# Windowed attention and a gated MLP on one core: four one-bank accumulators, more idle products and another order of the pieces at the start

## The chip, the core and the metric

The kernel runs on one core of a Trainium2 chip. The metric is device time in microseconds (us) from one execution; the profile is of one further execution and has its own time. Engines: TensorE (PE; PEld is its weight load), VectorE (DVE), ScalarE (ACT), GpSimd (POOL) and SyncE (SP), which issues nearly all DMAs.

## The reference

Attention over 8 entries (B), 8 heads, 576 positions and 64 columns a head. Heads 0 to 3 see a plain window of 32 positions back; heads 4 to 7 see 32 positions back at a distance of 4 (dilated). The result is the input of an MLP with a sigmoid gate.

```python
scores = scale * np.matmul(q, k.transpose(0, 1, 3, 2))
mask_plain = (rel >= 0) & (rel < window)
mask_dil = (rel >= 0) & (rel < window * dilation) & (rel % dilation == 0)
scores = np.where(masks[None, :, :, :], scores, -1000000000.0)
...
attn = np.exp(scores)
attn = attn / (np.sum(attn, axis=-1, keepdims=True) + 1e-09)
return np.matmul(attn, v).astype(np.float32)
...
x = np.ascontiguousarray(attn_out.transpose(0, 2, 1, 3)).reshape(B * S, H * D)
h = x @ w_in
g = h * (1.0 / (1.0 + np.exp(-1.702 * h)))
return (g @ w_out).astype(np.float32)
```

x is 4608 x 512, w_in 512 x 2048, w_out 2048 x 512. The weights come as 64-bit floats.

## The kernel before

**Pieces and their order.** The body of the kernel adds pieces of work to a plan (`Plan.add`, L49): each has a cost on every engine that could do it, an urgency, the keys that it reads and writes, and at times a slack. `Plan.ordered` (L69) then writes out the order by hand: it keeps a clock for each engine and for the DMA bus, takes the engine that can start first, and on it the piece of the lowest urgency among those that can start. Pieces whose urgency is below 4 (the first entry's) may be preferred though they start later by `AHEAD` times the cost (L104 to 110). The engines then run their queues in this order, each strictly in order. The costs, urgencies, slacks, `AHEAD` and `WARM` are the planner's numbers, not measurements, and act on the order alone. What an instruction waits for is worked out apart from the plan, from the tiles that it reads and writes.

**Attention.** A pair of heads is one unit, 32 pairs in all, 4 to each entry. Pair k loads q and k (`load_qk`, L308) and v (`load_v`, L322), multiplies scores in small 32-row blocks (`scores`, L354: masks at L361, products at L375) into the tile sp, takes a softmax over a window of 64 (`exponentials` and `softmax`, L378 to 423: L394 maximum, L398 exponential, L412 sum, L421 or L425 transposes; GpSimd or VectorE divide), and multiplies by v. The first entry (pairs 0 to 3) has a way of its own: `first_attention` (L529) with `first_product` (L446, L462), which writes x into the accumulators' tile, as it is not yet in use; `drain_x` (L478) takes x out, a rounded high part xh by ScalarE and the rest xl by VectorE. Later pairs go by `attention` (L538) and `product` (L467, L476) through the tile av.

**MLP.** Tokens go in nine groups: 512 of each entry, and the rest of all entries in one. Every float32 factor is split in a high and a low part, and three products stand for one. A group has 16 steps f: `up` (L586) multiplies 12 times (L597: 4 blocks c of x, 3 products) into the bank hp; ScalarE's tanh (L605), VectorE's gate (L608), a rounding (L226) and a subtraction (L233) make gh and gl; `down` (L627) adds 12 products (L633, L634 for gh, L637 for gl) to four accumulators j of 128 x 512, one PSUM bank each. TensorE's order is up(f+1), then down(f). In the last step, each accumulator is drained (L645; L226 by ScalarE, tile ost) and stored when its three products are through. The next group's first `down` begins them anew, after its `up(1)`. All four accumulators are one tile:

```python
accs = bank([P, NC, GT], "acc", "acc")
```

**Weights.** `decode` (L241) turns one 128 x 512 block of 64-bit weights into a high and a low float32 part: one DMA (L271), ScalarE copies (L281, L282, at times L275), VectorE integer work (L277, L285, L287), a rounding (L226 or L228) and a subtraction (L233, VectorE or GpSimd). 32 blocks (n even: w_in, n odd: w_out) are decoded during the first entry and the first group.

**Idle products.** Before a piece on TensorE that the plan expects later than TensorE is free, up to its time `WARM`, the plan puts products of the identity with itself (L719), of which nothing is read, as many as fit by a formula (L116). They are written into the bank hp, and only until the first group's first `up` has used it.

**DMA.** All loads stand in SP's queue in the plan's order. At the start these are qk of pairs 0 to 3, the first blocks of weights and v of pairs 0 to 3.

Of the kernel before, what the change touches and what calls it, by code (L numbers as in the profile page):

```python
# [22 lines left out]
AHEAD = 0.6  # L23
WARM = 30.0
# [10 lines left out]
LATER = {PE: 0.0, ACT: 0.0, DVE: 0.4, POOL: 0.0, DMA: 0.0}  # L35
# [3 lines left out]
class Plan:  # L39
# [29 lines left out]
    def ordered(self, warm, warm_until, soon):  # L69
# [24 lines left out]
        while any(open_):  # L94
# [19 lines left out]
            if e == PE and when < warm_until:  # L114

                idle = max(0, int((when - max(free[e], 1.2) - 1.5) / (0.28 if when > 5.0 else 0.44)))  # L116
                order.extend([(None, e)] * idle)
# [20 lines left out]
def tile_windowed_attention_then_gated_mlp(  # L138
# [49 lines left out]
    accs = bank([P, NC, GT], "acc", "acc")  # L188
# [52 lines left out]
    def decode(n, urgency):  # L241
# [38 lines left out]
        add({DMA: 524}, {0: -7.0, 1: -5.0, 2: -3.5, 3: -2.5}.get(n, urgency), fetch, (), (R, R + "l", *taken))  # L280
# [41 lines left out]
    def load_v(k):  # L322
        u, place = pairs[k], lots(k)[1]

        def work(e):
            if k < NC:
                n = (QT if dilated(k) else QT + 1) * 2 * D
                flat = (None, late, main_x, left_x)[k][:, 2 * S:2 * S + n] if k else temp([P, n], F32, "v", f"v_{k}")
                u["v"] = flat.rearrange("p (s a d) -> p s a d", a=2, d=D)

                load(flat, first_v[k][:, 2 * D * (QT + 1) - n:])
                return
            flat = late_v if place == "v1" else temp([P, 2 * nv], F32, "v", f"v_{k}")
            u["v"] = [flat[:, nv * a:nv * a + nv].rearrange("p (m d) -> p m d", m=NW) for a in range(2)]
            for a in range(2):
                load(u["v"][a][0:KW], vp[k - NC, :, a])

        add({DMA: 390 if k < NC else 442}, (-5.5, -3.0, -2.0, -1.0)[k] if k < NC else 1.6 * k - 0.3, work, waits(k),
            (place, place + "l"), (0.0, 6.0, 8.0, 10.0)[k] if k < NC else 0.0)
# [66 lines left out]
    def softmax(k, urgency):  # L406
# [7 lines left out]
        for a in range(2):  # L414
            add({POOL: 0.73, DVE: -0.48}, urgency, lambda e, a=a: pair(
                e, pr[:, a], pr[:, a], sm[:, a, :, None].broadcast_to([P, QT, W]), ALU.mult), (SM,), (f"{PR}.{a}",))
# [29 lines left out]
    def first_product(k):  # L446
# [6 lines left out]
        u["x"] = accs[:, :, ROW * (k % 2):ROW * (k % 2) + ROW]  # L453
# [24 lines left out]
    def drain_x(k, urgency):  # L478
# [19 lines left out]
        if b == 0:  # L498
# [8 lines left out]
            for n, (size, part, src) in enumerate(mains):  # L507
                add({ACT: 0.12 + size * 0.00094}, urgency, lambda e, part=part, src=src: copy(
                    e, part(xh[:, c]), src()), FOUR, (f"xh{c}.{n}",))
                add({DVE: 0.08 + size / 640}, urgency, lambda e, part=part, src=src: pair(  # L510
                    e, part(xl[:, c]), src(), part(f32(xh[:, c])), ALU.subtract), (*FOUR, f"xh{c}.{n}"), (f"xl{c}.{n}",))
# [17 lines left out]
    def first_attention(k, urgency):  # L529
# [3 lines left out]
        add({PE: 1.7}, urgency - 1.0e5, lambda e: scores(k), (lots(k)[0],), ("sp",))  # L533
        softmax(k, urgency)
        add({PE: 1.1}, urgency - 1.0e5, lambda e: first_product(k), (lots(k)[1], f"ct{k % 2}.0", f"ct{k % 2}.1"), FOUR)
# [29 lines left out]
    class Group:  # L565
# [20 lines left out]
        def up(self, f):  # L586
# [12 lines left out]
            for c in range(NC):  # L599
                split = [f"x{k}{c}.{n}" for k in "hl" for n in range(1)] if self is main[0] else []  # L600
# [26 lines left out]
        def down(self, f):  # L627

            def hi(j):
                if f == 0:  # L630
                    self.acc[j] = accs[:, j]
# [53 lines left out]
    for c in range(NC):  # L685
        first_attention(c, c)
        if c in (1, 2):
            decode(c - 1, c + 2.5)
    last, nxt = None, 1
    for g in groups:  # L690
        g.split_x()
        if nxt == 1:
            for n in range(2, 2 * NF - 8):
                decode(n, 25.0 + 2.3 * n)
# [6 lines left out]
        for f in range(NF):  # L701
            g.up(f)
            if nxt == 1 and f == 1:
                for c in range(NC):
                    attention(NC + c, 50.0 + 10.0 * c)
                for n in range(2 * NF - 8, 2 * NF):
                    decode(n, 25.0 + 2.3 * n)
# [7 lines left out]
    def warm(e):  # L715
        if 0 not in main[0].hps:
            if "idle" not in misc:
                misc["idle"] = bank([P, GT], "hp", "idle")
# [49 lines left out]
```

## Time and profile before

| what | value |
|---|---|
| median of 3 runs | 924.18 us (923.68 to 924.65) |
| the profiled execution's own time | 923.53 us |
| its span, first to last instruction | 921.8 us |
| mean granted TensorE clock | 0.990 |
| DMA | 61.32 MB, mean 67 GB/s |

Three stages can be told apart in the windows view by busy time: up to 40 us, the first entry's attention and the first decodes, with VectorE at 27.75 us and ScalarE at 25.89; from there to about 130 us, the first group beside the remaining decodes and the second entry's attention, with DVE and ACT nearly full; then the other eight groups, with TensorE full and DVE and ACT less than half used. Times in the views count from the span's start. A row of the timeline is: start, length, engine, line, operation, output and inputs, count, and in brackets the idle time of the engine before it and what ended it. Matmuls are pipelined: the start of the next, not the length of a row, tells the rate. In a row of waits stand the total, the number and the longest.

### The profile page before, as it was taken

The numbers are of one execution on the slowest core, as the hardware profiler recorded it, in microseconds if no ns is written. First come the engines' busy times: TensorE is split into PE (matmuls) and PEld (weight loads), VectorE is DVE, ScalarE is ACT, GpSimd is POOL, SyncE is SP. The second block draws the span as 40 slices with busy tenths as digits, with TensorE's granted clock in tenths as the row PEclk, the third lists the DMA queues.
The fourth block names the chain that finished last, engine by engine and source line by source line (L and its number), as shares of the span: only waits on it lengthen the run. The fifth ranks groups of instructions, "written<-read, shape, count | busy, mean of one in ns | idle before, by whom it ended". The sixth has DMA issues, their size and how long they took to land.

```text
span 921.8 us, 17123 instructions
## 1 busy us (share of the span) xinstructions
PE 888.0 (96%) x7313; PEld 714.7 (78%) x7313; DVE 450.3 (49%) x844; ACT 386.0 (42%) x669; POOL 71.7 (8%) x86
## 2 busy tenths in 40 slices
PE   6899999999999999999999999999999999999997
PEld 4577777888788878888788878887888778878885
DVE  6799985564556254634564255525422412232221
ACT  5889874343543244323443244424422322232222
POOL 3312220010001000000010000100000000000000
PEclk9799999999999999999999999999999999999999
DMA  9366742211221012300311023101000010001001
GB/s 347 126 223 179 246 134 91 92 46 46 91 92 46 1 64 73 92 0 16 122 46 47 1 91 91 46 1 44 24 1 1 2 44 1 1 14 32 1 1 46
DMA packets 35803, 61.32 MB, mean 67 GB/s; under 512 B 17424, under 2 KB 17680, under 8 KB 35728
## 3 DMA queue, kind: packets, MB, share of 16 engines
q1 hardware_dynamic: 35584, 60.11, 20.3%
q8 instruction: 57, 0.93, 0.4%
q14 instruction: 18, 0.15, 0.1%
q10 hardware_dynamic: 144, 0.13, 0.0%
HBM read 49.48 MB, written 9.44 MB: 64 GB/s over the span
## 4 chain that ended last, share of the span: by engine, by line
PE 90%; ACT 5%; DMA 2%; DVE 1%; issue 1%; SPq 0%; ACTq 0%
PE hp_m L597 37%; PE acc L637 14%; PE acc L633 14%; PE acc L634 13%; PE hp_r L597 5%; PE av L476 3%; PE sp L375 3%; ACT ost_m L226 2%; DMA cell<-wo_dram 1%; PE acc L462 1%; DMA cell<-wi_dram 1%; DMA second<-wo_dram 1%; ACT words L281 1%; ACT second L275 1%; ACT gh L226 0%
## 5 line engine op out<-in xcount | busy, mean ns | idle before, releaser
L633 PE MATMUL acc<-gh,woh 128*128 128x512 f32 x576 | 226.9, 394 | 4.9 <-ACT ost_m L226 4.1
L634 PE MATMUL acc<-gh,wol 128*128 128x512 f32 x576 | 224.4, 390 | 0.0
L597 PE MATMUL hp_m<-xh,wih 128*128 128x512 f32 x512 | 203.8, 398 | 2.8 <-ACT xh L226 1.9
L597 PE MATMUL hp_m<-xl,wih 128*128 128x512 f32 x512 | 201.4, 393 | 0.3 <-DVE xl L233 0.2
L597 PE MATMUL hp_m<-xh,wil 128*128 128x512 f32 x512 | 201.3, 393 | 0.0
L608 DVE SCALAR_TENSOR_TENSOR g_m<-g_m,hp_m 128x512 f32<-128x512 f32 x128 | 87.8, 686 | 230.3 <-ACT g_m L605 229.9
L637 PE MATMUL acc<-gl,woh 128*128 128x512 f32 x576 | 162.3, 394 | 13.7 <-ACT ost_m L226 11.7
L605 ACT ACTIVATE g_m<-hp_m 128x512 f32<-128x512 f32 x128 | 76.6, 599 | 234.4 <-PE hp_m L597 233.9
L637 PEld LDWEIGHTS acc<-gl,woh 128*128 128x128 f32 x576 | 107.6, 188 | 44.3 <-ACT ost_m L226 19.0
L633 PEld LDWEIGHTS acc<-gh,woh 128*128 128x128 f32 x576 | 108.1, 188 | 31.1 <-ACT ost_m L226 6.1
L634 PEld LDWEIGHTS acc<-gh,wol 128*128 128x128 f32 x576 | 108.2, 188 | 21.9
L233 DVE TENSOR_TENSOR gl<-g_m,gh 128x512 fp32r<-128x512 f32 x126 | 89.1, 707 | 58.1 <-ACT gh L226 52.9
L597 PEld LDWEIGHTS hp_m<-xh,wih 128*128 128x128 f32 x512 | 97.0, 190 | 25.5 <-DVE g_m L608 3.1
L597 PEld LDWEIGHTS hp_m<-xl,wih 128*128 128x128 f32 x512 | 97.2, 190 | 22.1 <-DVE xl L233 1.4
L597 PEld LDWEIGHTS hp_m<-xh,wil 128*128 128x128 f32 x512 | 97.1, 190 | 20.1 <-POOL wil L233 0.6
L226 ACT ACTIVATE gh<-g_m 128x512 fp32r<-128x512 f32 x117 | 73.9, 632 | 68.8 <-DVE g_m L608 68.6
L233 POOL TENSOR_TENSOR pr<-pr,sm 128x320 f32<-128x320 f32 x64 | 52.4, 840 | 520.8 <-DVE sm L404 516.6
L226 ACT ACTIVATE bt<-ct 32x320 f32<-32x320 f32 x101 | 47.5, 470 | 14.3 <-DVE ct L425 12.4
L226 ACT ACTIVATE xm<-av 128x512 f32<-128x512 f32 (+2 forms) x42 | 24.5, 594 | 44.8 <-PE av L476 31.5
L608 DVE SCALAR_TENSOR_TENSOR g_r<-g_r,hp_r 128x512 f32<-128x512 f32 x16 | 11.0, 688 | 53.6 <-ACT g_r L605 53.6
L398 ACT ACTIVATE pr<-pr 128x640 f32<-128x640 f32 x32 | 23.7, 740 | 30.9 <-DVE pr L233 30.8
L412 DVE TENSOR_REDUCE sm<-pr 128x10 f32<-128x640 f32 x32 | 26.2, 817 | 13.3 <-ACT pr L398 13.3
(114 smaller groups left out, 717.6 us busy)
## 6 DMA issues: line engine op xcount, KB each, us to landing
qk<-qk_dram SPq DMA_DIRECT2D x17, 576.0 KB, 4.8
out_dram<-ost_m SPq DMA_DIRECT2D x31, 256.0 KB, 2.0
second<-qk_dram SPq DMA_DIRECT2D x13, 576.0 KB, 4.3
v<-vp_dram SPq DMA_DIRECT2D x32, 216.0 KB, 4.3
words<-vp_dram SPq DMA_DIRECT2D x24, 216.0 KB, 4.4
cell<-wi_dram SPq DMA_DIRECT2D x10, 512.0 KB, 5.6
cell<-wo_dram SPq DMA_DIRECT2D x9, 512.0 KB, 4.4
second<-wo_dram SPq DMA_DIRECT2D x6, 512.0 KB, 5.2
```

The source lines that it names most:

```text
L226: A.activation(dst, src, AF.Copy, scale=scale)
L233: (V if e == DVE else G).tensor_tensor(out=dst, in0=a, in1=b, op=op)
L375: T.matmul(dst[:, w:w + n], u["qk"][rows, at:at + 32], u["qk"][rows, S + first:S + first + n], start=not masked(k), stop=True, tile_positi ...
L398: add({ACT: 0.75}, urgency, lambda e: A.activation(prs[y], prs[y], AF.Exp, scale=0.125), (), (PR,))
L412: add({DVE: 0.80}, urgency, lambda e: V.tensor_reduce(out=sm, in_=pr, axis=AX.X, op=ALU.add), (PR,), (SM,))
L476: T.matmul(dst, u["v"][a][0:KW, m], bt[0:KW, a, m], start=True, stop=True, skip_group_check=True)
L597: T.matmul(hps[f], st[:, f, c], mv[:, c], start=c == 0 and k == 0, stop=c == NC - 1 and k == 2)
L605: A.activation(self.g32, hps[f], AF.Tanh, scale=0.851)
L608: V.scalar_tensor_tensor(out=self.g32, in0=self.g32, scalar=1.0, in1=hps[f], op0=ALU.add, op1=ALU.mult)
L633: T.matmul(self.acc[j], woh[:, f, cols], gh, start=f == 0, stop=False)
L634: T.matmul(self.acc[j], wol[:, f, cols], gh, start=False, stop=False)
L637: T.matmul(self.acc[j], woh[:, f, P * j:P * j + P], self.g[f][1], start=False, stop=f == NF - 1)
```

## The change

The tile accs is replaced twice. The first entry's x is written to a tile first_x in a pool of its own, which is closed when the first accumulator is asked for; then a second pool gives each group four tiles of one bank (`quarter`). The idle products go to the bank av in place of hp, may go on until the first pair of the second entry uses it, up to planned time 36 in place of 30, and leave 0.5 us of a gap free in place of 1.5. In the plan, costs, urgencies and slacks of pieces change: loads and decodes of the first weights become more urgent, those of the later blocks less (28 + 2.62n for 25 + 2.3n), the second entry's attention more urgent (43 + 8.2c for 50 + 10c); the readiness of the v loads of pairs 1 to 3 goes from 6, 8, 10 to 1, 5, 14. `up` of the first group names the second part of a plain head pair's x among the keys that it reads. What is computed stays the same.

```diff
@@ -20,8 +20,8 @@
 NF = DF // P
 GT = 512
 LT = S - GT
-AHEAD = 0.6
-WARM = 30.0
+AHEAD = 0.70
+WARM = 36.0
 FIRST = 2
 NEG = -1.0e30
 QT = 5
@@ -32,7 +32,7 @@
 
 
 PE, ACT, DVE, POOL, DMA = range(5)
-LATER = {PE: 0.0, ACT: 0.0, DVE: 0.4, POOL: 0.0, DMA: 0.0}
+LATER = {PE: 0.0, ACT: 0.0, DVE: 0.40, POOL: 0.0, DMA: 0.0}
 LATENCY = {PE: 0.3, ACT: 0.2, DVE: 0.2, POOL: 0.2, DMA: 0.2}
 
 
@@ -113,7 +113,7 @@
             cost = abs(ops[i][0][e])
             if e == PE and when < warm_until:
 
-                idle = max(0, int((when - max(free[e], 1.2) - 1.5) / (0.28 if when > 5.0 else 0.44)))
+                idle = max(0, int((when - max(free[e], 1.2) - 0.5) / (0.26 if when > 8.0 else 0.44)))
                 order.extend([(None, e)] * idle)
             order.append((i, e))
             if e == POOL or (e == DVE and ops[i][0][e] < 0):
@@ -185,7 +185,15 @@
 
     bt = fixed([P, 2, NW + 1, D], F32, "bt")
 
-    accs = bank([P, NC, GT], "acc", "acc")
+    four = tc.tile_pool(name="four", bufs=1, space=bass.MemoryType.PSUM)
+    first_x = four.__enter__().tile([P, NC, GT], F32, tag="x", name="first_x")
+
+    def quarter(j, name):
+        if "quarters" not in misc:
+            four.__exit__(None, None, None)
+            misc["quarters"] = ctx.enter_context(tc.tile_pool(name="quarters", bufs=1, space=bass.MemoryType.PSUM))
+        return misc["quarters"].tile([P, GT], F32, tag=f"acc{j}", name=name)
+
 
     mask, plain = fixed([P, QT, W], BF16, "mask"), fixed([P, QT, W], BF16, "plain")
     ident = fixed([P, P], BF16, "ident")
@@ -277,7 +285,7 @@
                 V.tensor_scalar(out=at["halves"][:, :, 1], in0=at["halves"][:, :, 3], scalar1=0x8000, scalar2=None,
                                 op0=ALU.bitwise_and)
 
-        add({DMA: 524}, {0: -7.0, 1: -5.0, 2: -3.5, 3: -2.5}.get(n, urgency), fetch, (), (R, R + "l", *taken))
+        add({DMA: 524}, {0: -8.1, 1: -6.2, 2: -5.2, 3: -4.5}.get(n, urgency), fetch, (), (R, R + "l", *taken))
         add({ACT: 0.66}, urgency, lambda e: A.activation(value, f32(at["top"]), AF.Copy, scale=2.0 ** -112), (R,), (E,))
         add({ACT: 0.66}, urgency, lambda e: A.activation(
             at["low"], at["low"], AF.Copy, scale=2.0 ** -29), (R,), (R + "l",))
@@ -336,7 +344,7 @@
                 load(u["v"][a][0:KW], vp[k - NC, :, a])
 
         add({DMA: 390 if k < NC else 442}, (-5.5, -3.0, -2.0, -1.0)[k] if k < NC else 1.6 * k - 0.3, work, waits(k),
-            (place, place + "l"), (0.0, 6.0, 8.0, 10.0)[k] if k < NC else 0.0)
+            (place, place + "l"), (0.0, 1.0, 5.0, 14.0)[k] if k < NC else 0.0)
 
     def waits(k):
 
@@ -412,7 +420,7 @@
         add({DVE: 0.80}, urgency, lambda e: V.tensor_reduce(out=sm, in_=pr, axis=AX.X, op=ALU.add), (PR,), (SM,))
         inverse(k, urgency)
         for a in range(2):
-            add({POOL: 0.73, DVE: -0.48}, urgency, lambda e, a=a: pair(
+            add({POOL: 0.85, DVE: -0.48}, urgency, lambda e, a=a: pair(
                 e, pr[:, a], pr[:, a], sm[:, a, :, None].broadcast_to([P, QT, W]), ALU.mult), (SM,), (f"{PR}.{a}",))
         if k < NC:
 
@@ -450,7 +458,7 @@
 
         u = pairs[k]
         ct = cts[k % 2].rearrange("p h a t q -> p (h a t q)").rearrange("p (a n) -> p a n", a=2)
-        u["x"] = accs[:, :, ROW * (k % 2):ROW * (k % 2) + ROW]
+        u["x"] = first_x[:, :, ROW * (k % 2):ROW * (k % 2) + ROW]
         for s in range(QT + 1):
             at, to = max(W * s // 2 - 32, 0), min(32 * s + 32, ROW)
 
@@ -505,9 +513,9 @@
                          (GT - 3 * ROW, lambda x: x[:, 3 * ROW:], lambda: u["x"][:, 3, 0:GT - 3 * ROW])]
                 rests = [(lambda x: x, lambda: u["x"][:, 3, GT - 3 * ROW:])]
             for n, (size, part, src) in enumerate(mains):
-                add({ACT: 0.12 + size * 0.00094}, urgency, lambda e, part=part, src=src: copy(
+                add({ACT: 0.12 + size * (0.0019 if dilated(k) else 0.00094)}, urgency, lambda e, part=part, src=src: copy(
                     e, part(xh[:, c]), src()), FOUR, (f"xh{c}.{n}",))
-                add({DVE: 0.08 + size / 640}, urgency, lambda e, part=part, src=src: pair(
+                add({DVE: 0.08 + size / (490 if dilated(k) else 820)}, urgency, lambda e, part=part, src=src: pair(
                     e, part(xl[:, c]), src(), part(f32(xh[:, c])), ALU.subtract), (*FOUR, f"xh{c}.{n}"), (f"xl{c}.{n}",))
             for n, (part, src) in enumerate(rests):
                 add({ACT: 0.22, DVE: 0.2}, urgency, lambda e, part=part, src=src: copy(e, part(xr[:, b, c]), src()),
@@ -530,9 +538,9 @@
 
         load_qk(k)
         load_v(k)
-        add({PE: 1.7}, urgency - 1.0e5, lambda e: scores(k), (lots(k)[0],), ("sp",))
+        add({PE: 1.6 if k else 2.1}, urgency - 1.0e5, lambda e: scores(k), (lots(k)[0],), ("sp",))
         softmax(k, urgency)
-        add({PE: 1.1}, urgency - 1.0e5, lambda e: first_product(k), (lots(k)[1], f"ct{k % 2}.0", f"ct{k % 2}.1"), FOUR)
+        add({PE: 1.4}, urgency - 1.0e5, lambda e: first_product(k), (lots(k)[1], f"ct{k % 2}.0", f"ct{k % 2}.1"), FOUR)
         drain_x(k, urgency)
 
     def attention(k, urgency):
@@ -597,7 +605,7 @@
                     T.matmul(hps[f], st[:, f, c], mv[:, c], start=c == 0 and k == 0, stop=c == NC - 1 and k == 2)
 
             for c in range(NC):
-                split = [f"x{k}{c}.{n}" for k in "hl" for n in range(1)] if self is main[0] else []
+                split = [f"x{k}{c}.{n}" for k in "hl" for n in range(2)] if self is main[0] else []
                 add({PE: 0.681}, 0.0, lambda e, c=c: product(c), (f"wi{f}", f"xh{c}", f"xl{c}", *split), (place,))
 
             def tanh(e):
@@ -628,7 +636,7 @@
 
             def hi(j):
                 if f == 0:
-                    self.acc[j] = accs[:, j]
+                    self.acc[j] = quarter(j, f"acc_{self.name}_{j}")
                 gh, cols = self.g[f][0], slice(P * j, P * j + P)
                 T.matmul(self.acc[j], woh[:, f, cols], gh, start=f == 0, stop=False)
                 T.matmul(self.acc[j], wol[:, f, cols], gh, start=False, stop=False)
@@ -685,13 +693,13 @@
     for c in range(NC):
         first_attention(c, c)
         if c in (1, 2):
-            decode(c - 1, c + 2.5)
+            decode(c - 1, c + 0.1)
     last, nxt = None, 1
     for g in groups:
         g.split_x()
         if nxt == 1:
             for n in range(2, 2 * NF - 8):
-                decode(n, 25.0 + 2.3 * n)
+                decode(n, 28.0 + 2.62 * n)
             zeroed = [f"bt.{m}" for m in range(8)]
             add({POOL: 1.2}, 20.0, lambda e: G.memset(bt[0:KW], 0.0), (), ("bt", "btl", *zeroed))
             add({ACT: 0.5}, 30.0, lambda e: mask_dilated(), (), ("mask",))
@@ -702,9 +710,9 @@
             g.up(f)
             if nxt == 1 and f == 1:
                 for c in range(NC):
-                    attention(NC + c, 50.0 + 10.0 * c)
+                    attention(NC + c, 43.0 + 8.2 * c)
                 for n in range(2 * NF - 8, 2 * NF):
-                    decode(n, 25.0 + 2.3 * n)
+                    decode(n, 28.0 + 2.62 * n)
             if last:
                 last[0].down(last[1])
             last = g, f
@@ -713,9 +721,9 @@
 
 
     def warm(e):
-        if 0 not in main[0].hps:
+        if "av" not in pairs[NC]:
             if "idle" not in misc:
-                misc["idle"] = bank([P, GT], "hp", "idle")
+                misc["idle"] = bank([P, GT], "av", "idle")
             T.matmul(misc["idle"], ident, ident[:, None, :].broadcast_to([P, GT // P, P]), start=True, stop=True)
 
     for work, e in plan.ordered(warm, WARM, NC):
```

## The prediction, made before the changed kernel was run

> **What bounds the kernel now.** I read the page first, then the chain of waits, the waits of TensorE, and the timeline at one change of groups and over the start.
>
> ```profile
> PE 888.0 (96%) x7313; PEld 714.7 (78%) x7313; DVE 450.3 (49%) x844; ACT 386.0 (42%) x669; POOL 71.7 (8%) x86
> ```
> ```profile
> 50.93 2.72 PE hp_m L597 x12
> ```
> TensorE is busy 96% of the span, so the time is its products plus whatever holds it. In a dense stretch the chain gives 2.72 us for 12 products, 0.227 us each. What holds it stands in the waits of TensorE (total, times, longest):
>
> ```profile
> PE acc L637 <- ACT ost_m L226: 11.7, 17, 0.7
> PE acc L633 <- ACT ost_m L226: 4.1, 6, 0.7
> PE acc L637 <- ACT ost_r L226: 2.1, 3, 0.7
> ```
> These are 26 waits, 17.9 us, all for ScalarE's drain of a finished accumulator. The timeline at the first change of groups shows what they wait for:
>
> ```profile
> 138.44 0.39 PE L634 MATMUL acc<-gh,wol 128*128 128x512 f32 x1
> 138.86 0.60 ACT L226 ACTIVATE ost_m<-acc 128x512 f32<-128x512 f32 x1 [0.47 <-PE acc L634]
> ...
> 139.51 0.50 PE L637 MATMUL acc<-gl,woh 128*128 128x512 f32 x1 [0.69 <-ACT ost_m L226]
> ...
> 139.85 0.40 PE L633 MATMUL acc<-gh,woh 128*128 128x512 f32 x1
> ...
> 142.39 1.09 ACT L226 ACTIVATE ost_m<-acc 128x512 f32<-128x512 f32 x2 [0.76 <-PE acc L637]
> 142.42 0.39 PE L597 MATMUL hp_m<-xh,wil 128*128 128x512 f32 x1
> ```
> The drain of accumulator 0 starts only after the products of accumulator 1 (L634 at 138.44), and L637 of accumulator 1 then waits for the drain of accumulator 0. They share no data: they share the tile accs. At 142.39, by contrast, ScalarE drains acc while TensorE writes hp, another tile, and nobody waits. So the order is kept per tile.
>
> **The change, part by part.** *Four tiles in place of one.* No instruction is added. From L634 at 138.44 to L633 at 139.85 are two steps and 1.41 us; a dense stream takes 2 x 0.227 = 0.45, so one wait costs 0.96 us with the refill of the array. 26 x 0.96 = **25.0 us**, all on the engine that sets the end. What is late next: a group's first L633 on accumulator j must still find j drained. Between them lie the 12 products of the next step of L597, 2.72 us, and the drains, 0.60 us each, can follow accumulators that finish every 3 x 0.227 = 0.68 us; so ScalarE keeps pace, and the product that waits is 2.72 us behind. If that cover were gone, a drain would cost its 0.60 us once per group, 9 x 0.60 = 5.4 us at most; I take nothing.
>
> The pool that holds the first entry's x is closed before the four tiles open. TensorE's first product into them must wait for the last reader of x:
>
> ```profile
> 36.06 1.12 DVE L233 TENSOR_TENSOR xl<-acc,xh 128x512 fp32r<-128x512 f32 x1
> ```
> ```profile
> 41.73 0.50 PE acc L633
> ```
> It reads until 37.18, and the first L633 starts at 41.73 after gh: 4.5 us of cover, cost nothing.
>
> *The slow clock that the waits set off.* At one change of groups the pauses are followed by slow products:
>
> ```profile
> 645.08 0.63 PE L597 MATMUL hp_m<-xh,wil 128*128 128x512 f32 x1
> ...
> 648.07 0.47 PE L597 MATMUL hp_m<-xl,wih 128*128 128x512 f32 x1
> 648.38 0.39 PE L597 MATMUL hp_m<-xh,wih 128*128 128x512 f32 x1
> ```
> Eight steps take 648.38 - 645.08 = 3.30 us in place of 1.82: **1.5 us**, gone if the pauses go.
>
> *Idle products.* They now go on past the first use of hp, in the bank of av, and fill more of each gap. The start at present:
>
> ```profile
> 6.44 1.03 PE L719 MATMUL idle<-ident 128*128 128x512 bf16 x2
> ...
> 10.32 1.46 PE L719 MATMUL idle<-ident 128*128 128x512 bf16 x3
> ...
> 19.79 0.61 PE L462 MATMUL acc<-ct,v 32*64 32x48 f32 x21 [2.01 <-issue]
> 20.33 0.71 PE L361 MATMUL sp<-early,ident 128*128 128x320 bf16 x2
> ...
> 22.37 0.79 PE L597 MATMUL hp_m<-xh,wih 128*128 128x512 f32 x1
> ...
> 23.81 1.54 PE L462 MATMUL acc<-ct,second 32*64 32x32 f32 x92
> ...
> 31.18 0.79 PE L597 MATMUL hp_m<-xh,wih 128*128 128x512 f32 x1 [1.17 <-ACT xh L226]
> ...
> 33.20 1.54 PE L462 MATMUL acc<-ct,xr 32*64 32x64 f32 x80
> 34.67 0.80 PE L597 MATMUL hp_m<-xh,wih 128*128 128x512 f32 x1
> ...
> 38.04 0.39 PE L597 MATMUL hp_m<-xh,wih 128*128 128x512 f32 x1
> ```
> ```profile
> 46.60 0.45 PE L361 MATMUL sp<-plain,ident 128*128 128x320 bf16 x2
> 46.98 1.00 PE L375 MATMUL sp<-qk 64*32 64x32 f32 x76
> 47.91 0.50 PE L633 MATMUL acc<-gh,woh 128*128 128x512 f32 x1
> ```
> ```profile
> 27.00:37.25 10.25, 8.65 (x170) 6.25 (x171) 7.48 (x16) 8.98 (x12) 4.51 (x4) 0.50 0.40 143
> ```
> The last row is a stretch of the windows view (its busy times are PE, PEld, DVE, ACT, POOL; then granted clock, DMA share, GB/s): the clock stood at 0.50 from 27.00 to 37.25. The products at 22.37 are as slow, so I read the time before as slow too, by their durations. At full clock: scores with their mask took 47.91 - 46.60 = 1.31 us against 22.37 - 20.33 = 2.04 (0.7 saved); the three products from 22.37 to 23.81 take 0.68 in place of 1.44 (0.8); the third product of the group at 31.18 would let L462 go about 0.5 earlier than 33.20, bounded by the subtraction before it; the nine from 34.67 to 38.04 take 2.04 in place of 3.37 (1.3). These lie on the chain that leads to the first tanh: **3.3 us**. The small matmuls of L462 I leave as they are. Both ends: 0 (the clock stays low) and 3.3.
>
> The Trainium skill ("TensorE: Matmul & The Clock Gate", section on the HAM clock gate) says that the array runs at half rate until about 3.4 us of sustained activity and falls back after an idle window, the windows being free-running. The steps of 0.43 and 0.227 us here agree. By that rule, with gaps filled from the start, scores of the second and third pair would be fast as well.
>
> *Earlier weight loads and decodes.* The loads of the first weights move ahead of loads of qk on SP's queue (w_in's first before the second qk, the next three before the fourth qk, and the first two decodes come due with the second and third pair); loads of v move behind or wait for later starts (5 and 14 in the planner's time).
>
> ```profile
> 1.26 0.42 SPq L318 DMA_DIRECT2D second<-qk_dram  x1
> 1.72 0.43 SPq L271 DMA_DIRECT2D cell<-wi_dram  x1
> ```
> ```profile
> 8.13 0.67 ACT L281 ACTIVATE words<-cell 128x512 f32<-128x512 f32 x1 [2.91 <-DMA cell<-wi_dram]
> 8.71 0.67 ACT L282 ACTIVATE cell<-cell 128x512 uint32<-128x512 uint32 x1
> 9.28 0.72 ACT L398 ACTIVATE pr<-pr 128x640 f32<-128x640 f32 x1
> 12.13 0.67 ACT L281 ACTIVATE words<-cell 128x512 f32<-128x512 f32 x1 [2.13 <-DMA cell<-wo_dram]
> ```
> ```profile
> 0.00:40.00 40.00, 29.64 (x737) 18.91 (x737) 27.75 (x62) 25.89 (x42) 14.20 (x22) 0.87 0.66 242
> 40.00:100.00 60.00, 59.27 (x603) 46.59 (x604) 55.64 (x104) 53.40 (x84) 11.94 (x11) 1.00 0.69 217
> ```
> ScalarE idles 2.91 us for the first weights, then decodes them at 8.13 and 8.71, and the first pair's exponential (L398) stands behind until 9.28. Weights that land earlier take the decode out of its way: at most the two decodes, 1.15 us (8.13 to 9.28); I take **1.0**. The second qk, one transfer later, has cover: its scores ran behind the first pair's softmax. The other moves I cost at 0: VectorE idles 12.2 us and ScalarE 14.1 of the first 40, which hides a decode that comes early; without this cover a misplaced decode costs its row, 0.7 us, on either. The moved order could also win or lose up to VectorE's idle time from 40 to 100, 60 - 55.6 = 4.4 us, since attention of the second entry now comes due earlier and late decodes later there; I take 0, both ends go into the range.
>
> The profiled execution took 923.5 us (span 921.8 and 1.7 around it), 0.7 under the median of 924.18. Sum: 923.5 - 25.0 - 1.5 - 3.3 - 1.0 = **892.7 us**.
>
> **The rivals.**
> *The start's gain is swallowed.* From 40 to 100 VectorE is busy 93% and ScalarE 89%, on decodes and attention; if they, not TensorE, set the pace there, an earlier start only makes TensorE wait for weights. Against it: 4.4 and 6.6 us of idle time and an almost free GpSimd. Only the pauses are won: 923.5 - 26.5 = 897.0.
>
> *Idle products get in the way.* The planner now counts 0.26 us each after its time 8; two took 1.03 at 6.44 and three 1.46 at 10.32, so one more costs 0.43. A gap that gave 3 products by (gap - 1.5)/0.28 was at least 2.34 us, and gives 7 by (gap - 0.5)/0.26; one that gave 2, 6. One gap of the first kind and two of the second hold 19: 19 x (0.43 - 0.26) = 3.2 us too long, less the margin of 3 x 0.5: 1.7 us, if the clock stays low. And TensorE has more instructions to fetch: the pause of 2.01 at 19.79 waits for nothing that the profile shows, while loads fill the queues; a second one costs 2.0. Then 897.0 + 3.7 = 900.7. For it: that pause; against it: filled gaps raise the clock, and then 0.26 is right. The Trainium skill ("Runtime: NRT & Kernel Launch", section on instruction fetch) says blocks of 256 instructions are fetched ahead and mostly hidden; the pause speaks against "mostly" here, if it is a fetch, which no row proves.
>
> *Full clock from the second pair.* If the filled gaps raise the clock before the second pair's scores, two more sets of scores gain 0.7 each: 892.7 - 1.4 = 891.3; with the order winning its 4.4 too, 887. Against it: the idle products of now did not raise it by 22.37. The Trainium skill's clock rule, named above, would have it so.
>
> *The four tiles still wait on one another*, if the tiles' release goes by pool. The row at 142.39 speaks against it. Only the start is won: 923.5 - 4.3 = 919.2.
>
> *Slower than before.* TensorE takes its queue in order, and scores of the second entry's four pairs come due earlier. If each stood there before its qk had landed, every product behind would wait. To eat 30.8 us this takes 7.7 us for each of the four; below that the kernel is still faster. The loads of qk land in a median of 4.8 us by the page:
>
> ```profile
> qk<-qk_dram SPq DMA_DIRECT2D x17, 576.0 KB, 4.8
> ```
> The wait must thus be longer than a whole load, four times. At 10 us each the time would be 892.7 + 40 = 933.
>
> **How the numbers follow.** Forecast (start gains 2 to 6 us, 891 to 895) 0.42; swallowed, up to 899, 0.25; idle products in the way, to 904, 0.16; full clock early, down to 886, 0.08; tiles still waiting 0.05; slower 0.04. The range 886 to 903 leaves out the last two and the worst of the third, some 0.13. About 0.2% (1.8 us) is what a measurement here tells from no change: faster 0.94, same 0.02 (tiles still waiting and the start lost), slower 0.04.
>
> **What would show it.** Right: no wait of L633 or L637 for ost in TensorE's waits; L634 to L637 in one 0.227 us step at each change; no 0.63 us product past 50 us; the granted clock at 1.00 from 27 to 37; first exponential before 9 us; first tanh near 34.6 (38.93 now, by the chain's row below).
>
> ```profile
> 38.93 0.60 ACT g_m L605
> ```
> Wrong: such waits by another name; a stretch between 40 and 130 in which L597 waits for wih or wil; "issue" longer than 2.01 us on TensorE; idle products still running when the mask of a pair's scores could start.

## The result, and the profile after

| | before | changed |
|---|---|---|
| median | 924.25 us | 900.51 us (899.6 to 901.36, 4 runs) |
| ratio | | 0.9743, 95% interval 0.9727 to 0.976 |
| profiled execution, its span | 923.53, 921.8 us | 900.52, 898.4 us |

The kernel became 23.7 us faster; 31.5 were forecast by the medians. Below, L605 of the changed kernel is L597 of before, L641, L642 and L645 are L633, L634 and L637: its lines are 8 higher, and those of the experiments with four tiles 7 (8 in l_changed_44; d_idle_order has the lines of before). The first row of the profile's page and TensorE's longest waits:

```profile
PE 883.9 (98%) x7352; PEld 718.3 (80%) x7352; DVE 461.6 (51%) x858; ACT 390.1 (43%) x680; POOL 50.2 (6%) x61
```
```profile
PE hp_m L605 <- ACT woh L234: 2.2, 1, 2.2
PE first_x L470 <- issue: 1.9, 1, 1.9
PE idle L727 <- POOL ident L201: 1.5, 1, 1.5
PE sp L383 <- issue: 1.1, 1, 1.1
```

The 26 waits for a drain are gone; what is left lies in the first 44 us, but for 1.0 us in two waits between 126 and 134. A change of groups is now dense, as the timeline shows for the last step of the second group:

```profile
243.25 0.39 PE L641 MATMUL acc_m<-gh,woh 128*128 128x512 f32 x1
243.48 0.39 PE L642 MATMUL acc_m<-gh,wol 128*128 128x512 f32 x1
243.71 0.39 PE L645 MATMUL acc_m<-gl,woh 128*128 128x512 f32 x1
243.93 0.39 PE L641 MATMUL acc_m<-gh,woh 128*128 128x512 f32 x1
...
245.97 0.39 PE L605 MATMUL hp_m<-xh,wih 128*128 128x512 f32 x1
```

Twelve products fill 245.97 - 243.25 = 2.72 us, the dense rate, through all four accumulators. The start went the other way. The same milestone in both traces, the start of the first product of a step:

| step | before | changed | difference |
|---|---|---|---|
| first group, f = 0 | 22.37 | 24.35 | +2.0 |
| first group, f = 2 | 40.31 | 43.62 | +3.3 |
| second group, f = 0 | 134.81 | 139.25 | +4.4 |
| third group, f = 0 | 238.34 | 240.52 | +2.2 |
| fourth group, f = 0 | 337.86 | 336.97 | -0.9 |
| ninth group, f = 0 | 821.79 | 804.20 | -17.6 |
| end of the span | 921.8 | 898.4 | -23.4 |

From the second group's start to the end the changed kernel gains 27.8 us; up to there it had lost 4.4. A group's first product comes ahead of the drains of the group before it, so the last row holds the drains of two groups. The first gain is 2.2 us (two waits were there), the next is 3.1 (three waits), as are most. The changed kernel's start in the timeline (TensorE, then VectorE, then ScalarE) and in stretches of the windows view:

```profile
17.46 0.77 PE L470 MATMUL first_x<-ct,v 32*64 32x32 f32 x50 [0.67 <-DVE ct L429]
20.18 0.92 PE L470 MATMUL first_x<-ct,v 32*64 32x64 f32 x40 [1.95 <-issue]
...
24.18 0.24 PE L383 MATMUL sp<-xr 64*32 64x16 f32 x2 [1.09 <-issue]
...
27.52 3.17 PE L727 MATMUL idle<-ident 128*128 128x512 bf16 x8
30.34 0.59 PE L605 MATMUL hp_m<-xh,wih 128*128 128x512 f32 x1
...
43.62 0.62 PE L605 MATMUL hp_m<-xh,wih 128*128 128x512 f32 x1 [2.16 <-ACT woh L234]
```
```profile
7.20 0.43 DVE L293 TENSOR_SCALAR words<-words 128x512 uint32<-128x512 uint32 x1 [2.28 <-ACT words L289]
7.54 0.82 DVE L402 TENSOR_REDUCE mx<-sp 128x10 f32<-128x640 f32 x1
```
```profile
9.79 0.72 ACT L406 ACTIVATE pr<-pr 128x640 f32<-128x640 f32 x1
...
40.80 0.60 ACT L613 ACTIVATE g_m<-hp_m 128x512 f32<-128x512 f32 x1
```
```profile
19.00:30.00 11.00, 8.73 (x231) 5.61 (x231) 6.14 (x16) 6.40 (x13) 2.11 (x3) 0.54 0.41 149
30.00:40.00 10.00, 9.23 (x191) 6.24 (x190) 8.32 (x18) 9.78 (x12) 2.13 (x2) 0.99 0.40 122
44.00:47.00 3.00, 3.00 (x8) 2.29 (x8) 3.00 (x7) 2.06 (x4) 0.00 (x0) 0.50 0.77 229
```

VectorE's first maximum (L402) now stands behind a decode's shift that waits for ScalarE, 7.54 in place of 6.54; the first exponential runs at 9.79 in place of 9.28; a second pause without a releaser has come in at 24.18; the first tanh starts at 40.80 in place of 38.93. The clock is full from 30, but half in most of 19 to 30 and again from 44 to 47, after the pause of 2.16.

Why the product at 43.62 comes 3.3 us late can be followed back on TensorE and VectorE:

```profile
31.77 1.08 PE L470 MATMUL first_x<-ct,xm 32*64 32x64 f32 x80
```
```profile
30.11 0.90 DVE L429 STREAM_TRANSPOSE ct<-pr 128x320 f32<-128x320 f32 x2
...
34.16 0.68 DVE L295 CUSTOM_DVE_ANT_0 words<-cell,words 128x1024 uint16<-128x1024 uint16 x1
34.75 1.08 DVE L241 TENSOR_TENSOR xl<-first_x,xh 128x512 fp32r<-128x512 f32 x1
...
38.30 0.91 DVE L236 CAST woh<-words 128x512 fp32r<-128x512 f32 x1
39.13 1.07 DVE L241 TENSOR_TENSOR xl<-first_x,xh 128x512 fp32r<-128x512 f32 x1
...
42.17 0.71 DVE L295 CUSTOM_DVE_ANT_0 words<-second,words 128x1024 uint16<-128x1024 uint16 x1
42.80 0.68 DVE L616 SCALAR_TENSOR_TENSOR g_m<-g_m,hp_m 128x512 f32<-128x512 f32 x1
```

The third pair's transposes end at 31.01 (30.11 + 0.90), but its product starts at 31.77, 0.7 us after it could: ahead of it in TensorE's queue stand the eight idle products of 27.52, the three products that waited behind them, and two more idle ones. Then three times a decode's piece stands in VectorE's queue ahead of a piece that the chain waits for: 0.6 us ahead of the subtraction at 34.75, 0.8 ahead of that at 39.13, and 1.4 ahead of the gate at 42.80, as tanh had ended at 41.40. In the kernel before the two subtractions (31.30 and 36.06) and the gate (39.57) follow at once on what they need. The four together are 3.5 us. That is an estimate: the pauses ahead of them (the first product is 2.0 late) and the faster products from 30 on come on top, with opposite signs. The profile puts the pause of 2.16 down to the rounding of woh on ScalarE, which ends at 43.55; the gate ended at 43.48.

### The profile page after: what moved, and what is told of

Read it like the earlier page. It is cut to its first block, busy times and chain, and to the rows that moved or that the text cites. A ratio compares the mean times of both kernels' runs of the same rounds, so it can differ in the third digit from the quotient of the medians.

```text
span 898.4 us, 17202 instructions
## 1 busy us (share of the span) xinstructions
PE 883.9 (98%) x7352; PEld 718.3 (80%) x7352; DVE 461.6 (51%) x858; ACT 390.1 (43%) x680; POOL 50.2 (6%) x61
## 4 chain that ended last, share of the span: by engine, by line
PE 92%; ACT 3%; DMA 2%; DVE 2%; issue 1%; SPq 0%; DVEq 0%; ACTq 0%
PE hp_m L605 38%; PE acc_m L641 13%; PE acc_m L642 13%; PE acc_m L645 12%; PE hp_r L605 5%; PE av L484 3%; PE sp L383 3%; PE acc_r L642 2%; PE acc_r L641 2%; PE acc_r L645 2%; DMA cell<-wi_dram 1%; DMA second<-wi_dram 1%; ACT words L289 0%; PE first_x L470 0%; PE sp L484 0%
## 5 line engine op out<-in xcount | busy, mean ns | idle before, releaser
L605 PE MATMUL hp_m<-xh,wih 128*128 128x512 f32 x512 | 201.5, 394 | 2.9 <-ACT woh L234 2.2
L641 PE MATMUL acc_m<-gh,woh 128*128 128x512 f32 x512 | 201.6, 394 | 0.3 <-ACT gh L234 0.3
L605 PE MATMUL hp_m<-xh,wil 128*128 128x512 f32 x512 | 200.1, 391 | 0.0
L605 PE MATMUL hp_m<-xl,wih 128*128 128x512 f32 x512 | 199.9, 391 | 0.0
L642 PE MATMUL acc_m<-gh,wol 128*128 128x512 f32 x512 | 199.8, 390 | 0.0
L645 PE MATMUL acc_m<-gl,woh 128*128 128x512 f32 x512 | 143.4, 391 | 0.0
L605 PEld LDWEIGHTS hp_m<-xh,wih 128*128 128x128 f32 x512 | 96.2, 188 | 24.6 <-ACT woh L234 2.6
L641 PEld LDWEIGHTS acc_m<-gh,woh 128*128 128x128 f32 x512 | 96.5, 189 | 21.4 <-ACT gh L234 0.7
L605 PEld LDWEIGHTS hp_m<-xl,wih 128*128 128x128 f32 x512 | 96.4, 188 | 20.4 <-DVE xl L241 0.3
L605 PEld LDWEIGHTS hp_m<-xh,wil 128*128 128x128 f32 x512 | 96.4, 188 | 20.2 <-DVE wil L241 0.7
L642 PEld LDWEIGHTS acc_m<-gh,wol 128*128 128x128 f32 x512 | 96.6, 189 | 19.7
L645 PEld LDWEIGHTS acc_m<-gl,woh 128*128 128x128 f32 x512 | 95.5, 188 | 20.1
L234 ACT ACTIVATE gh<-g_m 128x512 fp32r<-128x512 f32 x113 | 71.2, 630 | 67.5 <-DVE g_m L616 67.4
L241 POOL TENSOR_TENSOR pr<-pr,sm 128x320 f32<-128x320 f32 x45 | 40.1, 901 | 546.6 <-DVE sm L412 541.8
L406 ACT ACTIVATE pr<-pr 128x640 f32<-128x640 f32 x32 | 23.7, 740 | 41.1 <-DVE pr L241 40.5
L234 ACT ACTIVATE xm<-av 128x512 f32<-128x512 f32 (+2 forms) x42 | 23.7, 596 | 28.8 <-PE av L484 16.6
```

Of the source, the lines that this page charges most:

```text
L234: A.activation(dst, src, AF.Copy, scale=scale)
L241: (V if e == DVE else G).tensor_tensor(out=dst, in0=a, in1=b, op=op)
L406: add({ACT: 0.75}, urgency, lambda e: A.activation(prs[y], prs[y], AF.Exp, scale=0.125), (), (PR,))
L605: T.matmul(hps[f], st[:, f, c], mv[:, c], start=c == 0 and k == 0, stop=c == NC - 1 and k == 2)
L641: T.matmul(self.acc[j], woh[:, f, cols], gh, start=f == 0, stop=False)
L642: T.matmul(self.acc[j], wol[:, f, cols], gh, start=False, stop=False)
```

## The experiments

Each kernel was timed in turns with the kernel before, and its ratio to that is what is compared; 0.001 is 0.92 us. Four runs came first, the tiles alone and the three parts of the change in twos.

| kernel | tiles | idle | order | median | ratio (95% interval) |
|---|---|---|---|---|---|
| a_tiles | new | old | old | 898.08 | 0.9702 (0.9685 to 0.9718) |
| b_tiles_idle | new | new | old | 897.70 | 0.9705 (0.9689 to 0.9721) |
| c_tiles_order | new | old | new | 899.31 | 0.9722 (0.9705 to 0.9739) |
| changed | new | new | new | 900.51 | 0.9743 (0.9727 to 0.976) |
| d_idle_order | old | new | new | 927.93 | 1.0037 (1.0022 to 1.0052) |

**a_tiles.** The kernel before with only these edits (quarter as in the change):

```diff
-    accs = bank([P, NC, GT], "acc", "acc")
+    first_x = four.__enter__().tile([P, NC, GT], F32, tag="x", name="first_x")
-        u["x"] = accs[:, :, ...
+        u["x"] = first_x[:, :, ...
-                    self.acc[j] = accs[:, j]
+                    self.acc[j] = quarter(j, f"acc_{self.name}_{j}")
```

> The kernel before with the four one-bank tiles alone; idle products and order as before. In the changed kernel the distance to the kernel before goes from +4.4 us at the first product of the second group to -23.4 at the end, so the tiles are worth 27.8 us there and the rest of the change lost 4.4. Theory 1 (the order of the pieces lost it) and theory 2 (the idle products lost it) both give 924.2 - 27.8 = 896.4 here. A rival to both, that the tiles themselves delay the first group (the closed pool, the new tile of each group): 900.5 here, as in the changed kernel.

898.08, ratio 0.9702: the tiles alone are worth 27.6 us (0.0298 x 924.9), and more than the whole change; the two intervals do not meet. The rival that the tiles account for the lost start falls with it. In the one trace of a_tiles the second group does start 1.8 us later than in the one of before (136.65 for 134.81); whether that is the tiles or the spread between runs (896.8 to 898.55 here) is not shown.

**d_idle_order.** The changed kernel without these edits.

> The changed kernel with its accumulators in one tile as before: idle products and order changed, tiles not. If the parts add up: 900.5 + 27.8 = 928.3, slower than the kernel before by 4 us. If the tiles also took part in the loss at the start: 924 or less.

927.93: idle products and order without the tiles lose 3.4 us (0.0037 x 924.9), clear of no change by the interval. The waits are all there again:

```profile
PE acc L637 <- ACT ost_m L226: 11.0, 16, 0.7
PE acc L633 <- ACT ost_m L226: 4.8, 7, 0.7
PE acc L637 <- ACT ost_r L226: 2.1, 3, 0.7
```

The parts add up: the changed kernel's ratio is 0.0294 lower, 27.2 us, which is what the tiles are worth with the other two parts in place.

**b_tiles_idle.** a_tiles with the changed idle products:

```diff
-WARM = 30.0
+WARM = 36.0
-    idle = max(0, int((when - max(free[e], 1.2) - 1.5) / (0.28 if when > 5.0 else 0.44)))
+    idle = max(0, int((when - max(free[e], 1.2) - 0.5) / (0.26 if when > 8.0 else 0.44)))
-        if 0 not in main[0].hps:
+        if "av" not in pairs[NC]:
-                misc["idle"] = bank([P, GT], "hp", "idle")
+                misc["idle"] = bank([P, GT], "av", "idle")
```

> Four tiles and the changed idle products (bank of av, planned time 36, 0.5 us margin), order and planner's numbers of before. Theory 1 (the order lost the start): 896.4 less up to 3.3 us for the clock, 893 to 896.4. Theory 2 (the idle products stand in the way and lengthen the instruction stream): 900.5.

897.70, the same as a_tiles within the intervals, and between the two theories. The gain of up to 3.3 for the clock did not come, though the clock did: the products from 34.64 on take the dense step. What the gain met (ScalarE, VectorE and TensorE in the timeline of b_tiles_idle; L612 is tanh, L615 the gate):

```profile
37.47 0.60 ACT L612 ACTIVATE g_m<-hp_m 128x512 f32<-128x512 f32 x1
```
```profile
38.50 0.69 DVE L294 CUSTOM_DVE_ANT_0 words<-second,words 128x1024 uint16<-128x1024 uint16 x1
39.10 0.69 DVE L615 SCALAR_TENSOR_TENSOR g_m<-g_m,hp_m 128x512 f32<-128x512 f32 x1
```
```profile
39.85 0.62 PE L604 MATMUL hp_m<-xh,wih 128*128 128x512 f32 x1 [1.82 <-DVE g_m L615]
40.38 0.79 PE L604 MATMUL hp_m<-xh,wil 128*128 128x512 f32 x1
```

Tanh runs 1.5 us earlier than before (37.47 for 38.93), but its result at 38.07 waits a microsecond in VectorE's queue behind a decode; the gate starts at 39.10 (39.57 before). TensorE pauses 1.82 us, and the products behind the pause are slow again. Of tanh's 1.5 us, 0.46 are left at the product behind the pause (39.85 for 40.31), and none at the fourth product of that step (45.13 for 44.56).

**c_tiles_order.** a_tiles with the changed costs, urgencies, slacks, AHEAD and keys, as in the diff of the change.

> Four tiles and the changed order (costs, urgencies, slacks, AHEAD), idle products as before (bank of hp, planned time 30, 1.5 us margin). Theory 1 (the order lost the start): 900.5 or more, since the clock then is low as well. Theory 2 (the idle products lost it): 896.4 or less.

899.31, ratio 0.9722: 0.0020 above a_tiles, 1.8 us. The whole loss against a_tiles (0.0041, 3.8 us) is clear of the intervals. Neither theory's time came. By the ratios the order alone makes about half of it, and the idle products, worth nothing with the old order, the other 1.9 us with the new one; but the interval of c_tiles_order meets those of a_tiles and of the changed kernel, so the halves are not certain. Its trace has two of the decodes ahead of a subtraction as well (on VectorE at 32.52 and 37.06), so these come from the order.

The next three runs split the order; b_tiles_idle is what they are measured against.

**e_early_weights.**

```diff
-{0: -7.0, 1: -5.0, 2: -3.5, 3: -2.5}
+{0: -8.1, 1: -6.2, 2: -5.2, 3: -4.5}
-(0.0, 6.0, 8.0, 10.0)[k] if k < NC
+(0.0, 1.0, 5.0, 14.0)[k] if k < NC
-            decode(c - 1, c + 2.5)
+            decode(c - 1, c + 0.1)
```

> Four tiles and the changed idle products, and of the new order only the start: first weights' loads earlier, v loads' slacks, first two decodes with the second and third pair. The kernel without this start is b_tiles_idle, 897.7; with the whole order it is 900.5. Theory O1 (weights that land earlier put VectorE's decode work ahead of the first pairs' softmax): 899.5 to 900.5, with the first maximum near 7.5 us in place of 6.3. Theory O2 (the later due times of decodes and attention) and O3 (the planner's costs): 897.7 here, or 1.0 less as the prediction had it.

899.48, ratio 0.9721 (0.9709 to 0.9734): 1.5 us slower, as O1 had it, though the intervals of the two meet. Its mechanism is not there: the first maximum starts at 6.81, not 7.5. The loss shows elsewhere, in TensorE's waits:

```profile
PE first_x L469 <- issue: 3.6, 1, 3.6
PE acc_m L640 <- ACT gh L233: 1.9, 1, 1.9
```

**f_costs.**

```diff
-AHEAD = 0.6
+AHEAD = 0.70
-{POOL: 0.73, DVE: -0.48}
+{POOL: 0.85, DVE: -0.48}
...
-for n in range(1)] if self is main[0]
+for n in range(2)] if self is main[0]
```

(and the costs of scores, first product and first drains)

> Four tiles and the changed idle products, and of the new order only the planner's costs, AHEAD and the second part of x among the keys; loads, first decodes and due times as before. In the changed kernel GpSimd is busy 50 us in place of 72 and VectorE 462 in place of 450: divisions moved to VectorE. Theory O3 (these costs load VectorE while it sets the pace): 899.5 to 900.5, with GpSimd near 50 us. O1 and O2: 897.7.

899.88, ratio 0.9727 (0.9715 to 0.9739): 2.0 us slower, again with intervals that meet. The profile's page shows the divisions that went to VectorE:

```profile
PE 882.4 (98%) x7354; PEld 717.0 (80%) x7354; DVE 461.3 (51%) x858; ACT 389.6 (43%) x682; POOL 50.9 (6%) x59
```

**g_due_times.**

```diff
-decode(n, 25.0 + 2.3 * n)
+decode(n, 28.0 + 2.62 * n)
-attention(NC + c, 50.0 + 10.0 * c)
+attention(NC + c, 43.0 + 8.2 * c)
```

> Four tiles and the changed idle products, and of the new order only the due times of the later blocks and of the second entry's attention (28 + 2.62n, 43 + 8.2c). Theory O2 (weights come too late for the first group): 899.5 to 900.5. O1 and O3: 897.7.

903.07, ratio 0.9761 (0.9749 to 0.9773): 5.2 us slower, more than O2 had. The largest piece is one wait of TensorE, and what led to it on ScalarE:

```profile
92.19 0.50 PE L604 MATMUL hp_m<-xh,wih 128*128 128x512 f32 x1 [3.77 <-DVE g_m L615]
```
```profile
88.56 0.67 ACT L289 ACTIVATE second<-second 128x512 uint32<-128x512 uint32 x1 [2.03 <-DMA second<-wi_dram]
...
90.74 0.67 ACT L612 ACTIVATE g_m<-hp_m 128x512 f32<-128x512 f32 x1
```

A decode whose load had not landed stood in ScalarE's queue, with two more decode pieces behind it, ahead of a tanh; the gate and TensorE's next product followed late. Each part alone is slower than b_tiles_idle: 1.5 + 2.0 + 5.2 = 8.7 us, of which only the 5.2 is clear of the intervals, where the whole order on top of b_tiles_idle costs 3.5 (0.9743 - 0.9705). So they do not add up; the likely reason, not shown, is that each changes where the planner puts everything behind it.

**h_idle_44.** b_tiles_idle with `WARM = 44.0`.

> b_tiles_idle with idle products allowed up to planned time 44 in place of 36: 10 more stand ahead of the third step's first product, where TensorE waited 1.82 us for the gate at 39.85 and the clock then stood at half until 43.5. If the clock lost there is on the bound: 0.5 to 1.0 us less than 897.7, 897. If VectorE sets the pace there: 897.7. If they overrun the gate: up to 1 us more, 898.7.

896.47 (895.01 to 897.5, 6 runs), ratio 0.9692 (0.968 to 0.9704): 1.2 us less by the ratios, and the lowest median of the study. Its interval is apart from that of the changed kernel, but meets those of b_tiles_idle and a_tiles. Ten idle products fill the pause, and the granted clock stays full behind it (1.00 from 40 to 100):

```profile
37.43 2.33 PE L726 MATMUL idle<-ident 128*128 128x512 bf16 x10
39.45 0.55 PE L604 MATMUL hp_m<-xh,wih 128*128 128x512 f32 x1
39.98 0.50 PE L604 MATMUL hp_m<-xh,wil 128*128 128x512 f32 x1
```

**l_changed_44.** The changed kernel with `WARM = 44.0`.

> The changed kernel with idle products allowed up to planned time 44 in place of 36: 10 more stand in the 2.16 us pause after 41.06, behind which the clock stood at half from 43.8 to 47.2. Theory C (the pause drops the clock, and the clock is on the bound): about 1.2 us less than the changed kernel, as h_idle_44 against b_tiles_idle, 899.3 by the kernel before's 924.3. If the order's own delay sets the pace there, no gain: 900.5.

899.99, ratio 0.973 (0.9714 to 0.9745): 0.0013 less than the changed kernel, as theory C had it, but inside the intervals. In its profile nothing is slow behind the filled pause, yet the first product of the third step starts at 44.72, later than 43.62, behind longer pauses (4.9 us together, 3.0 in the changed kernel):

```profile
PE sp L383 <- issue: 3.1, 1, 3.1
PE first_x L470 <- issue: 1.8, 1, 1.8
```

**i_off_vector.** h_idle_44 with the planner's `LATER[DVE]` at 0.7 in place of 0.4.

> h_idle_44 with VectorE's handicap in the planner 0.7 in place of 0.4 us, so that pieces which another engine can do go there more often (GpSimd divides and subtracts more). If VectorE sets the pace of the first 140 us, its busy time there falls from 119 us and the end comes 1 to 3 us earlier: 893.5 to 895.5. If ScalarE or the chain between the engines sets it (GpSimd takes 0.9 us where VectorE takes 0.5): 896.5 or more, up to 899.

900.84, ratio 0.9739 (0.9722 to 0.9756): 4.3 us slower. From 40 to 100 VectorE is a little freer and GpSimd twice as busy (order of the columns: PE, PEld, DVE, ACT, POOL):

```profile
40.00:100.00 60.00, 58.84 (x602) 45.46 (x601) 54.50 (x85) 55.27 (x89) 23.31 (x19) 0.99 0.70 207
```

For h_idle_44 this stretch has DVE 55.15, ACT 53.35 and POOL 11.13. Taking work from VectorE did not help. But the edit took only 0.65 us of 55 from it, and gave ScalarE more; and the start was also held by 4.8 us of pauses (3.1 in h_idle_44). So whether VectorE's load sets the pace stays open.

**k_later_loads.** h_idle_44 with a slack of 18 on the fetch of blocks 4 and up.

> h_idle_44 with the loads of weight blocks 4 and up held back to planned time 18, so that the loads of the first 18 us are 2 MB fewer. In h_idle_44 TensorE stands still for 3.1 us in two pauses of the first product (issue), which end after the instruction queue's transfers. If those transfers wait behind the loads: pauses under 1.0 us together, the first product of the MLP near 19.5 in place of 20.86, and 895 to 896.5 at the end, as the later decodes take some of it back. If the pauses have another cause: 3 us of pauses as now.

936.06, ratio 1.0125 (1.0105 to 1.0145). The edit did more than was meant: the planner adds a slack behind every dependency, so each later load was planned 18 us behind the moment when its buffer was free, and TensorE waited for weights all through the first group. On the pauses it says half of what was asked:

```profile
18.61 0.66 PE L469 MATMUL first_x<-ct,v 32*64 32x64 f32 x33 [1.54 <-issue]
...
23.15 1.15 PE L469 MATMUL first_x<-ct,second 32*64 32x32 f32 x91 [0.28 <-issue]
```

The first pause stayed, the second all but went. As loads of v moved up into the room, the first 18 us carried as many bytes as in h_idle_44 (6.3 MB), so whether loads hold up the first pause was not tried by this run.

**m_loads_only.** h_idle_44 with the first two edits of e_early_weights, without the decodes' urgencies.

> h_idle_44 with the earlier loads of the first weights and the v loads' new slacks alone; the first two decodes keep their urgencies 3.5 and 4.5 of before. If weights that land earlier are in the way only because their decode comes due with the second and third pair (decode's urgency): first maximum on VectorE near 6.3 us, and 896.5 or up to 1 less. If landing earlier is enough to put the decode ahead: first maximum near 7.5 and 898 to 898.5.

899.47, ratio 0.9727 (0.9712 to 0.9742): 3.2 us slower than h_idle_44, clear of the intervals, and neither branch: the first maximum starts at 6.87. The first product starts earlier, as the prediction wanted (15.09; 15.65 in h_idle_44), and then stops:

```profile
15.09 0.86 PE L469 MATMUL first_x<-ct,v 32*64 32x32 f32 x61
20.33 0.45 PE L469 MATMUL first_x<-ct,v 32*64 32x48 f32 x31 [4.38 <-issue]
```

**What the pauses are.** Counting the matmul records ahead of the first such pause gives the same number in all 14 traces: in the kernel before 9 idle, 6 mask, 264 scores and 71 of the first product, 350; in m_loads_only 19 + 6 + 264 + 61, 350. Ten of the traces have a second one; it comes after number 478, 128 later (in a_tiles after 477). Each matmul has a weight load, so that is 256 instructions. The trace also holds the transfers of the instruction queue, of 16 KB each; the page of the changed kernel counts 58, for 2 x 7352 matmuls and weight loads, 254 to each:

```profile
q8 instruction: 58, 0.95, 0.5%
```

| kernel | idle ahead | matmul 350 starts | 16 KB transfer ends | matmul 351 starts | from transfer to 351 |
|---|---|---|---|---|---|
| before | 9 | 17.48 | 18.42 | 19.79 | 1.37 |
| a_tiles | 9 | 16.96 | 17.54 | 18.85 | 1.31 |
| h_idle_44 | 21 | 16.65 | 17.23 | 18.71 | 1.48 |
| e_early_weights | 23 | 15.67 | 17.91 | 19.45 | 1.54 |
| m_loads_only | 19 | 15.74 | 18.85 | 20.33 | 1.48 |
| changed | 28 | 18.02 | 18.64 | 20.18 | 1.54 |

TensorE stands at a fixed place of its instruction stream until a transfer has landed, and goes on 1.3 to 1.5 us later (1.2 to 1.5 in the 14 traces). What reaches that place earlier waits longer there. The transfer itself also lands later with the earlier weights: at 17.91 to 18.85 in the six kernels that have them, at 17.15 to 17.70 in seven of the other eight (18.42 in the kernel before). What holds it up is not shown. The Trainium skill ("Runtime: NRT & Kernel Launch", section on instruction fetch) gives blocks of 256 instructions in 16 KB; the 128 matmuls between the two pauses agree. It calls the cost of crossing a block mostly hidden; here only two of some 58 show, but these two, in the first 25 us, lasted up to 5.2 us (e_early_weights, 3.6 and 1.6).

## Why the prediction was right, and where it was not

The forecast was 892.7 us, and 900.51 was measured. The large part of the sum, the tiles, was right. The start, which was to gain 4.3 us, lost 3.8 against the tiles alone; the range held because it reached up to the rival "idle products get in the way".

- **The tiles** (25.0 us, and 1.5 for the slow clock behind the pauses, 26.5 together): right in mechanism and size. From the second group's first product to the end 26.8 us (a_tiles) and 27.8 (changed) were measured. No wait took the place of the old one: drains ran behind the accumulators, and the cover of the closed pool held.
- **The clock at the start** (3.3 us): the step failed. That the terms "lie on the chain that leads to the first tanh" was right, and tanh came 1.5 us earlier in b_tiles_idle; but the sum let this pass to the end. A decode ahead of the gate in VectorE's queue took back a microsecond of it, and the half clock behind TensorE's pause the rest. Alone the idle products were worth 0 (0.9705 against 0.9702); with the pause behind tanh filled too, 0.9 to 1.6 us (h_idle_44 against a_tiles, by ratios and by medians), which is inside the intervals. One term was read a little high: its 0.7 us for the scores set 76 products of a later pair against 88. At full clock the mask and 88 took 1.41 us (8.07 to 9.48 in b_tiles_idle), so 0.6.
- **Earlier weights** (1.0 us): wrong in sign. In the changed kernel the decode went ahead of the first maximum and the exponential came later (9.79 for 9.28), not earlier. In e_early_weights and m_loads_only the exponential ran at 8.89 and 8.93 (9.16 and 8.65 in the kernels that they are measured against), and the first product did start earlier (15.06 and 15.09 for 16.59 and 15.65); TensorE then waited for its instructions. They lose 1.5 and 3.2 us.
- **The other moves at 0**, with ends of 4.4 us on both sides: due times alone cost 5.2, costs 2.0, all of the order together 3.5 on top of the idle products. The end of the loss was the right one to keep, and too short for the due times.
- **The rivals.** The time was that of "idle products get in the way" (900.7). That it fits so closely is luck: a second pause did come, but of 1.09 us where it priced 2.0, and idle products did stand in the way, by 0.7 us at 31.77 where it priced 1.7; the decodes in VectorE's queue, 2.8 us by the rows above, are not in it. "Swallowed" (897.0) is what the tiles with the new idle products and the old order did (897.7). "The four tiles still wait" and "slower" are refuted, by the waits and by the time; the changed start alone is slower than before (d_idle_order), by 3.4 us and not by waiting for qk.
- **The signs named in advance.** Waits for ost gone, dense steps at the changes of groups: seen, and so was the full clock from 50 us on. First exponential before 9 (9.79), first tanh near 34.6 (40.80), full clock from 27 (from 30): not seen. Two signs of error came in part: "issue" above 2.01 only as a sum (1.95 + 1.09), and once, by 0.3 us, idle products were still running when a mask could start (VectorE lets go of the scores' tile at 9.21, the mask starts at 9.62).

Why the three parts of the order together cost less than alone, and whether data loads delay the instruction transfers, stays open.

## What to carry to other kernels

When a wait joins two engines that touch different data, look at whether they share a tile: split tiles by what is drained on its own, and price it as waits plus refill; that held to 5%. A gain on an engine in the start of a kernel is only worth what the next queue passes on: follow it past tanh to the gate before it goes into the sum. A plan tuned by hand is not a sum of its parts: change one part, measure, and keep the best (here tiles, idle products and the old order, 896.5; by the intervals it is not apart from the tiles alone).

## What the runs showed of the hardware that was not expected

TensorE stopped after its 350th and in ten of 14 traces after its 478th (once its 477th) matmul, whatever the program did. It went on 1.2 to 1.5 us after 16 KB of instructions had landed at the first of these stops; idle products that keep the clock up use the same stream. A pause of 1.8 to 2.2 us behind dense work was followed by 3 us at half clock (b_tiles_idle, changed), and ten idle products in it kept the clock full (h_idle_44). The Trainium skill ("TensorE: Matmul & The Clock Gate", section on the HAM clock gate) puts the fall after an idle window of about 3.4 us; here a shorter pause was enough.
